# Reordering the first dense layer's first pass: contraction outermost over seven open banks, W1 in row slabs from two queues

## The chip, the cores and the metric

The kernel runs on one core of a Trainium2 chip. The core has a matrix engine (TensorE, PE in the profile; its weight loads are PEld), a vector engine (VectorE, DVE), an activation engine (ScalarE, ACT), a general engine (GpSimd, POOL) and a queue engine (SyncE, SP). Transfers are issued by SP, ACT and POOL and run on 16 DMA engines. The metric is the device time of one execution in microseconds: 227.01 us for the kernel before, the median of three runs (226.88 to 227.04).

## The reference

The input `x` has 2048 rows (time steps) of 640 columns in bf16. Two branches read it, and a gate mixes them row by row:

```
g   = sigmoid(sum(x * gate_w))                         # one number per row
# branch A: a diagonal complex recurrence over the 2048 rows
Bu  = x @ B_bar.T                                      # complex, 640 states
h_t = Lam_bar * h_{t-1} + Bu_t
a   = 2 * Re(h @ C.T) + x * Dskip
# branch B: a dense layer pair, 640 -> 1728 -> 640
b   = gelu(x @ w1 + b1) @ w2 + b2
out = g * a + (1 - g) * b
```

## The kernel before

**Tiling.** The 2048 rows are worked in four quarters q of 512. In each quarter there are four kinds of TensorE work. `m1(q)` (L612, matmuls in L622) multiplies W1 with the transposed x: the hidden dimension of 1728 is cut into NF = 14 groups of 128 (the last has 64), the contraction of 640 into KD = 5 blocks of 128. For each group `jf` five matmuls of 128x128 by 128x512 add into one PSUM bank of 512 columns, then ACT takes the bank through a gelu into `Gl` (L629). `bproj(q)` (L634, L643) does the same with the two parts of B: ten groups of five matmuls, which ACT evicts into `U` (L652). `m2` (L718) and `cproj` (L742) work on 128 rows each: the second dense layer from `Gl` and W2, and the output projection from the state `H` and C; ACT evicts both into `E1` and `E2`, VectorE adds them up and SP stores the rows. Between `bproj` and `cproj` VectorE runs the recurrence (`ssm`, L657) in blocks of 256 rows: products with tables that it builds at the start, a scan (L683), products again, giving `H`.

**PSUM.** There are eight banks. `m1` and `bproj` take banks 0 to 3 in rotation (`BK_IN`), `m2` banks 4 and 5, `cproj` banks 6 and 7. So `m1` closes a group, and moves on to the next bank, every five matmuls.

**Start.** The transposed x of the first quarter is made on TensorE: two loads of 256 rows each fill `xn[0]`, twenty transposes (L410, in four groups of five, one group per 128 rows) write it to PSUM, VectorE copies each group to `xT` (L418). The other three quarters of `xT`, and B and C, are loaded by transposing DMAs (`load_T`, L331). Seven matmuls on a zero tile (L388) run ahead of everything on TensorE. `cols` (L430) and `colb` (L442) transpose small parameter rows into columns; the bias column of the gelu, `b1col`, comes from `colb`. ACT loads a function table ahead of Exp, of Sin and of gelu.

**Loads.** SP issues, in this order: the two x loads, W1 in three column pieces (columns 0 to 256, 256 to 896, 896 to 1728, all 640 rows each), ten transposes of B, five transposes for the rest of `xT`, W2 in two pieces, ten transposes of C, then the stores. ACT issues five small loads. POOL issues b2, the broadcasts `dsk` and `gwb` (one row of 1280 bytes to all 128 partitions each), and x of the second quarter in untransposed form (`xnload`, L339), later the two other quarters.

**What sets the order.** Each piece of work is an `op` (L170) with an engine, an estimated duration, what it reads and writes, and a priority. `Sched.order` (L53) runs a list schedule in estimated time: on each engine the ready item of lowest priority number goes first. From it comes one fixed order for each engine. `Emitter.wait` (L116) puts semaphore waits in front of an item for what it depends on. An item that takes several instructions marks only its end.

Of the kernel before, what the change touches and what calls it, by code (L numbers as in the profile page):

```python
# [9 lines left out]
BF16 = mybir.dt.bfloat16  # L10
I32 = mybir.dt.int32
ACT = mybir.ActivationFunctionType
# [135 lines left out]
class Prog:  # L148
# [8 lines left out]
    def op(self, name, eng, dur, reads, writes, fn, prio=None, lat=0.0, after=()):  # L157
        deps = {}
        for k in reads:
            for w in self.last_w.get(k, ()):  # L160
                deps[w.idx] = w
        for k in writes:
            for w in self.last_w.get(k, ()):
                deps[w.idx] = w
            for r in self.last_r.get(k, ()):
                deps[r.idx] = r
        for a in after:
            deps[a.idx] = a
        deps = list(deps.values())
        E = self.E  # L170

        def run(eg, deps=deps, eng=eng, fn=fn):
            E.wait(eng, *[d.done for d in deps])
            return fn()

        it = self.sch.add(name, eng, dur, deps, run, prio=prio, lat=lat)
        for k in writes:
            self.last_w[k] = [it]
            self.last_r[k] = []
        for k in reads:  # L180
            self.last_r.setdefault(k, []).append(it)
        return it


def bass_gated_mix__ssm_conv_s5__dense_activation_gelu__prompt_kernel(
# [18 lines left out]
    _, S, D = A_x.shape  # L204
    P = A_Lambda_re.shape[0]
    F = B_w1.shape[1]
    assert S % 512 == 0 and D % 128 == 0 and P == D
    KD = D // 128
    KP = P // 128
    NQ = S // 512  # L210
# [3 lines left out]
    NF = (F + 127) // 128  # L214
    FL = F - (NF - 1) * 128
# [6 lines left out]
    x2 = A_x[0]  # L222
# [3 lines left out]
    with ExitStack() as es, nc.Block() as block:  # L226
# [4 lines left out]
        xT = SB("xT", [128, KD, S], BF16)  # L231
        xn = [SB(f"xn_{i}", [128, 4, D], BF16) for i in range(2)]
        W1sb = SB("W1sb", [128, KD, F], BF16)
        W2sb = SB("W2sb", [128, NF, D], BF16)
        BT = SB("BT", [128, KD, 2, P], BF16)
        CT = SB("CT", [128, KP, 2, D], BF16)
        Gl = [SB(f"Gl_{i}", [128, NF, 512], BF16) for i in range(2)]
        dsk = SB("dsk", [128, D], BF16)
        gwb = SB("gwb", [128, D], BF16)
        b1col = SB("b1col", [128, NF], FP32)  # L240
        rows = SB("rows", [KP, 3, 128], BF16)
        b1rows = SB("b1rows", [NF, 128], BF16)
        lcol = SB("lcol", [128, 3, KP], FP32)
# [8 lines left out]
        ident = SB("ident", [128, 128], BF16)  # L252
# [53 lines left out]
        def inc(eng, ins):  # L306
            return E.inc(eng, ins, eng + "_s")
# [8 lines left out]
        def d_act(n):  # L316
            return 0.26 + n * 0.00084
# [4 lines left out]
        def d_mm(n):  # L322
            return n / 2400.0 + 0.004


        def load(name, eng, sem, dst, src, writes, prio, dur=0.5, lat=2.5, reads=(), **kw):
            def fn():
                return dma_inc(eng, engines[eng].dma_start(dst, src), sem)  # L328
            return op(name, eng, dur, reads, writes, fn, prio=prio, lat=lat)

        def load_T(name, sem, pairs, writes, prio, dur, lat=3.0):  # L331
            def fn():
                t = None
                for dst, src in pairs:
                    t = dma_inc("sp", nc.sync.dma_start_transpose(dst, src), sem)
                return t
            return op(name, "sp", dur, (), writes, fn, prio=prio, lat=lat)
# [5 lines left out]

        for h in range(2):
            load(f"x0_{h}", "sp", f"l_x0{h}", xn[0][:, 2 * h:2 * h + 2, :],
                 x2[h * 256:(h + 1) * 256, :].rearrange("(c p) d -> p c d", p=128), [("xn", 0, h)], prio=h, lat=2.0 + h)
        W1P = [(0, 256), (256, 896), (896, F)]
        for i, (f0, f1) in enumerate(W1P):
            load(f"w1_{i}", "sp", f"l_w1{i}", W1sb[:, :, f0:f1], B_w1[:, f0:f1].rearrange("(k p) f -> p k f", p=128),
                 [("w1", i)], prio=2 + i, lat=3.0 + i)  # L350
        nmain = (NF - 1) * 128

        def f_b1z():
# [30 lines left out]

        def f_warm():
            t = None
            for _ in range(7):
                t = nc.tensor.matmul(PS[BK_C[1]][:, :], wz[:, 0:128], wz[:, :], start=True, stop=True)  # L388
            return inc("pe", t)

        op("warm", "pe", 3.0, ["wz"], [("bank", BK_C[1])], f_warm, prio=-1000)

        def f_ones():
            inc("dve", nc.vector.memset(Gl[0][64:65, NF - 1, :], 1.0))
            return inc("dve", nc.vector.memset(Gl[1][64:65, NF - 1, :], 1.0))

        op("ones", "dve", 1.1, (), ["gl1"], f_ones, prio=-40)
        load("b2", "pool", "l_b2", W2sb[64:65, NF - 1, :], B_b2.rearrange("(o n) -> o n", o=1), ["b2"], prio=-30, dur=1.0)
        load("dsk", "pool", "l_dsk", dsk[:, :], A_Dskip.partition_broadcast(128), ["dsk"], prio=-29, dur=1.0)
        load("gwb", "pool", "l_gwb", gwb[:, :], gate_w.partition_broadcast(128), ["gwb"], prio=-28, dur=1.0)  # L400


        for c in range(4):
            bank = BK_IN[c]

            def f_tp(c=c, bank=bank):
                ps = PS[bank][:, :].bitcast(BF16)
                t = None
                for k in range(KD):
                    t = nc.tensor.transpose(ps[:, k * 128:(k + 1) * 128], xn[0][:, c, k * 128:(k + 1) * 128], ident[:, :])  # L410
                return inc("pe", t)

            op(f"tp{c}", "pe", 0.5, [("xn", 0, c // 2), "ident"], [("bank", bank)], f_tp, prio=-900 + c)

            def f_tpe(c=c, bank=bank):
                ps = PS[bank][:, :].bitcast(BF16)[:, 0:KD * 128].rearrange("p (k t) -> p k t", k=KD)
                dst = xT[:, :, c * 128:(c + 1) * 128]
                return inc("dve", nc.vector.tensor_copy(out=dst, in_=ps))  # L418

            op(f"tpe{c}", "dve", 0.5, [("bank", bank)], [("xT", 0, c)], f_tpe, prio=-2000 + c)  # L420
        XT = {q: [("xT", q)] for q in range(1, NQ)}
        XT[0] = [("xT", 0, c) for c in range(4)]


        psC = PS[BK_C[0]][:, :].bitcast(BF16)

        def f_cols():
            t = None
# [1 line left out]
                t = nc.tensor.transpose(psC[:, i * 8:i * 8 + KP], rows[:, i, :], ident[0:KP, 0:KP])  # L430
            return inc("pe", t)

        op("cols", "pe", 0.3, [("rows", 0), ("rows", 1), ("rows", 2), "ident"], [("bank", BK_C[0])], f_cols, prio=-897.5)

        def f_cols1():
            return inc("dve", nc.vector.tensor_copy(out=lcol[:, :, :], in_=psC[:, 0:24].rearrange("p (a k) -> p a k", a=3)[:, :, 0:KP]))

        op("cols1", "dve", 0.2, [("bank", BK_C[0])], ["lcol"], f_cols1, prio=-1000)
        psD = PS[BK_M2[0]][:, :].bitcast(BF16)

        def f_colb():
            return inc("pe", nc.tensor.transpose(psD[:, 0:NF], b1rows[:, :], ident[0:NF, 0:NF]))  # L442

        op("colb", "pe", 0.1, ["b1a", "b1b", "ident"], [("bank", BK_M2[0])], f_colb, prio=-896)

        def f_colb1():
            return inc("dve", nc.vector.tensor_copy(out=b1col[:, :], in_=psD[:, 0:NF]))

        op("colb1", "dve", 0.2, [("bank", BK_M2[0])], ["b1col"], f_colb1, prio=-1000)

        def f_dt():
            return inc("act", nc.scalar.activation(dtb[:, :], lcol[:, 2, :], ACT.Exp))
# [115 lines left out]
        def f_atab():  # L568
# [4 lines left out]
        op("atab", "dve", 1.5, ["amag"], ["atab"], f_atab, prio=-946)  # L573


        load_T("xT_rest", "l_xT", [(xT[:, k, 512:S], x2[512:S, k * 128:(k + 1) * 128]) for k in range(KD)],
               [("xT", q) for q in range(1, NQ)], prio=7, dur=13.0)
        load_T("B", "l_B", [(BT[:, k, ci, :], (A_B_re, A_B_im)[ci][:, k * 128:(k + 1) * 128]) for k in range(KD) for ci in range(2)],
               ["BT"], prio=6, dur=13.1)
        load("w2a", "sp", "l_w2a", W2sb[:, 0:NF - 1, :], B_w2[0:nmain, :].rearrange("(j p) d -> p j d", p=128), ["w2a"], prio=8, lat=8.0)  # L580
        load("w2b", "sp", "l_w2b", W2sb[0:FL, NF - 1, :], B_w2[nmain:F, :], ["w2b"], prio=9, lat=4.0)
        load_T("C", "l_C", [(CT[:, k, ci, :], (A_C_re, A_C_im)[ci][:, k * 128:(k + 1) * 128]) for k in range(KP) for ci in range(2)],
               ["CT"], prio=10, dur=14.0)

# [2 lines left out]
        def pe_prio():  # L587
            ctr["pe"] += 1
            return ctr["pe"]
# [19 lines left out]
            op(f"g{q}", "dve", 0.3, [("gth", q)], [("g", q)], fn3, prio=-100)  # L609


        def m1(q):  # L612
            for jf in range(NF):
                bank = BK_IN[ctr["in"] % 4]
                ctr["in"] += 1
                n = 128 if jf < NF - 1 else FL
                wp = [i for i, (f0, f1) in enumerate(W1P) if f0 <= jf * 128 < f1][0]

                def f_mm(jf=jf, bank=bank, n=n):
                    t = None  # L620
                    for k in range(KD):
                        t = nc.tensor.matmul(PS[bank][0:n, :], W1sb[:, k, jf * 128:jf * 128 + n], xT[:, k, q * 512:(q + 1) * 512],  # L622
                                             start=(k == 0), stop=(k == KD - 1))
                    return inc("pe", t)

                op(f"m1_{q}_{jf}", "pe", KD * d_mm(512), XT[q] + [("w1", wp)], [("bank", bank)], f_mm, prio=pe_prio())

                def f_ge(jf=jf, bank=bank, n=n):
                    return inc("act", nc.scalar.activation(Gl[q % 2][0:n, jf, :], PS[bank][0:n, :], ACT.Gelu_apprx_tanh, bias=b1col[0:n, jf:jf + 1]))  # L629

                op(f"ge_{q}_{jf}", "act", d_act(512), [("bank", bank), "b1col"], [("gl", q % 2, jf)], f_ge, prio=10)
# [170 lines left out]
                cproj(c)  # L802
                comb(c)

        m1(0)
        bproj(0)
        ssm(0)
        gates(0)
# [84 lines left out]
```

## Time and profile before

The profiled execution took 227.38 us, with a span of 225.6 us from its first instruction to its last.

| engine | busy, us | share of the span |
|---|---|---|
| TensorE, matmuls | 218.3 | 97% |
| TensorE, weight loads | 124.8 | 55% |
| VectorE | 191.6 | 85% |
| ScalarE | 101.5 | 45% |
| GpSimd | 4.8 | 2% |

TensorE's matmul time by kind: `m1` 65.8 us (280 matmuls), `m2` 63.6 (448), `cproj` 46.1 (320), `bproj` 43.8 (200). A matmul's recorded duration is longer than its distance from the next one, since matmuls are pipelined; the distance is what counts in a stream. A busy share is an average over the whole span: the first 14 us of the span look unlike the rest, and the granted TensorE clock, shown as a share of full speed, is not the same throughout. HBM read 7.38 MB and written 2.62 MB.

### The profile page before, as it was taken

How to read it: one execution, taken by the hardware profiler on the slowest of the kernel's cores; microseconds unless marked ns; L12 is line 12 of the kernel's file. 1: busy time of each engine (PE TensorE's matmuls, PEld its weight loads, DVE VectorE, ACT ScalarE, POOL GpSimd, SP SyncE). 2: the span in 40 equal slices, each digit the busy share in tenths (PEclk: the TensorE clock that was granted, in tenths of full speed). 3: DMA queues.
4: the chain of work that ended last, by engine and by line, in shares of the span. 5: the costliest groups of instructions: out<-in, count | busy, mean ns of one | idle time of the engine just before them, and what ended most of it. 6: DMA issues, size and time to landing. Idle time of an engine off the chain costs nothing.

```text
span 225.6 us, 3268 instructions
## 1 busy us (share of the span) xinstructions
PE 218.3 (97%) x1279; PEld 124.8 (55%) x1279; DVE 191.6 (85%) x267; ACT 101.5 (45%) x170; POOL 4.8 (2%) x14
## 2 busy tenths in 40 slices
PE   7589999999999999999999999999999999999995
PEld 3224444444457777544447777644446777777773
DVE  4799999799996999999999559999999999894312
ACT  2385655666553233455663223455663332323320
POOL 5000000000000010000000010000000000000000
PEclk9659999999999999999999999999999999999999
DMA  5997699977100023000000003000000000000000
GB/s 165 314 260 150 121 202 237 292 146 99 29 0 3 29 48 127 32 0 0 0 3 0 31 32 116 29 29 0 3 0 3 0 29 32 29 29 32 29 29 29
DMA packets 28631, 15.44 MB, mean 68 GB/s; under 512 B 21834, under 2 KB 28170, under 8 KB 28618
## 3 DMA queue, kind: packets, MB, share of 16 engines
q1 hardware_dynamic: 28000, 12.95, 25.1%
q0 software_dynamic: 560, 2.30, 3.5%
q8 instruction: 10, 0.16, 0.3%
q14 instruction: 3, 0.02, 0.0%
q10 hardware_dynamic: 58, 0.01, 0.0%
HBM read 7.38 MB, written 2.62 MB: 44 GB/s over the span
## 4 chain that ended last, share of the span: by engine, by line
PE 93%; DMA 5%; SPq 1%; DVE 0%; issue 0%
PE ps L718 27%; PE ps L622 27%; PE ps L742 19%; PE ps L643 19%; DMA W1sb<-in_B_w_dram 5%; SPq L328 1%; DVE osb L775 0%
## 5 line engine op out<-in xcount | busy, mean ns | idle before, releaser
L622 PE MATMUL ps<-xT,W1sb 128*128 128x512 bf16 (+1 forms) x280 | 65.8, 397 | 1.8 <-DVE tr L474 1.1
L718 PE MATMUL ps<-W2sb,Gl 128*128 128x320 bf16 x448 | 63.6, 299 | 0.0
L718 PEld LDWEIGHTS ps<-W2sb,Gl 128*128 128x128 bf16 x448 | 43.6, 98 | 18.0 <-issue 0.8
L622 PEld LDWEIGHTS ps<-xT,W1sb 128*128 128x128 bf16 (+1 forms) x280 | 28.1, 102 | 38.7 <-issue 6.6
L629 ACT ACTIVATE Gl<-ps,b1col 128x512 bf16<-128x512 f32 (+1 forms) x56 | 38.5, 687 | 24.5 <-PE ps L622 24.5
L742 PE MATMUL ps<-CT,H 128*128 128x320 bf16 x320 | 46.1, 299 | 0.0
L683 DVE TENSOR_TENSOR_SCAN W<-atab,V 128x1280 bf16<-128x1280 f32 x16 | 44.3, 2811 | 0.3
L643 PE MATMUL ps<-xT,BT 128*128 128x512 bf16 x200 | 43.8, 379 | 0.0
L742 PEld LDWEIGHTS ps<-CT,H 128*128 128x128 bf16 x320 | 31.3, 98 | 12.3
L652 ACT ACTIVATE U<-ps 128x512 bf16<-128x512 f32 x40 | 23.9, 597 | 19.4 <-PE ps L643 19.4
L643 PEld LDWEIGHTS ps<-xT,BT 128*128 128x128 bf16 x200 | 19.4, 98 | 23.6 <-issue 0.8
L761 DVE SCALAR_TENSOR_TENSOR xg<-xn,gcol,dsk 128x640 bf16<-128x640 bf16 x16 | 14.0, 883 | 0.5
L726 ACT ACTIVATE E_0<-ps,g1col 128x320 bf16<-128x320 f32 x12 | 6.3, 527 | 16.5 <-PE ps L718 15.1
L596 DVE SCALAR_TENSOR_TENSOR scr<-xn,gwb 128x640 bf16<-128x640 bf16 x16 | 13.2, 823 | 0.4
L492 DVE TENSOR_TENSOR V<-mr,U 128x2560 bf16<-128x2560 bf16 x8 | 11.9, 1489 | 1.7 <-ACT U L652 1.5
L492 DVE TENSOR_TENSOR V<-V,W 128x1280 bf16<-128x1280 bf16 x16 | 12.5, 821 | 0.3
L492 DVE TENSOR_TENSOR H<-H,V 128x1280 bf16<-128x1280 bf16 x16 | 12.5, 821 | 0.3
L492 DVE TENSOR_TENSOR H<-c,W 128x2560 bf16<-128x2560 bf16 x8 | 11.9, 1489 | 0.2
L492 DVE TENSOR_TENSOR W<-mi,U 128x2560 bf16<-128x2560 bf16 x8 | 11.9, 1484 | 0.0
L492 DVE TENSOR_TENSOR V<-s,W 128x2560 bf16<-128x2560 bf16 x8 | 11.9, 1484 | 0.0
L726 ACT ACTIVATE E_1<-ps,g1col 128x320 bf16<-128x320 f32 x10 | 5.3, 528 | 13.7 <-PE ps L718 13.7
L726 ACT ACTIVATE E_2<-ps,g1col 128x320 bf16<-128x320 f32 x10 | 5.3, 527 | 13.7 <-PE ps L718 13.7
(87 smaller groups left out, 90.4 us busy)
## 6 DMA issues: line engine op xcount, KB each, us to landing
out_dram<-osb SPq DMA_DIRECT2D x15, 160.0 KB, 1.8
W2sb<-in_B_w_dram SPq DMA_DIRECT2D x1, 2080.0 KB, 10.8
xn<-in_A_x_dram POOLq DMA_DIRECT2D x3, 640.0 KB, 4.6
W1sb<-in_B_w_dram SPq DMA_DIRECT2D x1, 1040.0 KB, 13.7
W1sb<-in_B_w_dram SPq DMA_DIRECT2D x1, 800.0 KB, 11.6
xn<-in_A_x_dram SPq DMA_DIRECT2D x2, 320.0 KB, 3.3
W1sb<-in_B_w_dram SPq DMA_DIRECT2D x1, 320.0 KB, 6.9
dsk<-in_A_Dskip_dram POOLq DMA_DIRECT2D x1, 160.0 KB, 6.4
```

The source lines that it names most:

```text
L328: return dma_inc(eng, engines[eng].dma_start(dst, src), sem)
L492: return inc("dve", nc.vector.tensor_tensor(out=o, in0=a, in1=b, op=o_))
L596: t = inc("dve", nc.vector.scalar_tensor_tensor(out=scr[:, :], in0=xn[q % 2][:, c, :], scalar=1.0, in1=gwb[:, :], op0=ALU.mult, op1=ALU.mu ...
L622: t = nc.tensor.matmul(PS[bank][0:n, :], W1sb[:, k, jf * 128:jf * 128 + n], xT[:, k, q * 512:(q + 1) * 512], start=(k == 0), stop=(k == KD ...
L629: return inc("act", nc.scalar.activation(Gl[q % 2][0:n, jf, :], PS[bank][0:n, :], ACT.Gelu_apprx_tanh, bias=b1col[0:n, jf:jf + 1]))
L643: t = nc.tensor.matmul(PS[bank][:, :], BT[:, kd, ci, k * 128:(k + 1) * 128], xT[:, kd, q * 512:(q + 1) * 512], start=(kd == 0), stop=(kd = ...
L652: return inc("act", nc.scalar.activation(dst, src, ACT.Copy, scale=1.0 if ci == 0 else -1.0))
L683: t = inc("dve", nc.vector.tensor_tensor_scan(out=g[:, ci, :], data0=a, data1=v[:, ci, :], initial=0.0, op0=ALU.mult, op1=ALU.add))
L718: t = nc.tensor.matmul(PS[bank][:, 0:HALF], Gl[q % 2][0:n, jf, t4 * 128:(t4 + 1) * 128], W2sb[0:n, jf, cols], start=(jf == 0), stop=(jf == ...
L726: return inc("act", nc.scalar.activation(E1[c % NE][:, cols], PS[bank][:, 0:HALF], ACT.Copy, scale=g1col[:, c:c + 1]))
L742: t = nc.tensor.matmul(PS[bank][:, 0:HALF], H[b % NHB][:, ci, k, s * 128:(s + 1) * 128], CT[:, k, ci, cols], start=(i == 0), stop=(i == 2 ...
L761: return inc("dve", nc.vector.scalar_tensor_tensor(out=xg[c % 2][:, :], in0=xn[q % 2][:, c % 4, :], scalar=gcol[:, c:c + 1], in1=dsk[:, :] ...
```

## The change

The first quarter's `m1` is split. `m1_first` does hidden groups 0 to 6 with the contraction block `k` as the outer loop: for each `k`, seven matmuls, one into each of banks 0 to 6, so that seven groups are open at once and all close in the last round. Groups 7 to 13 follow as before (`m1(0, NW)`). W1's columns 0 to 896 come as five row slabs of 128 rows, one for each `k`; slabs 0, 2, 4 on SP's queue, 1 and 3 on ACT's; the rest of W1 is one load on SP. The transposes of x are grouped by `k` rather than by rows, so that each bank holds one `k`; three of the five copies to `xT` are VectorE's and two ScalarE's. The zero-tile matmuls ahead become six instead of seven, and two more are put after each half of the transposes (`filler`). `colb` moves behind the second slab's matmuls. `b2`, `dsk` and `gwb` are issued only after the first matmul of slab 1 (`late`), which leaves POOL's x load as its first. On SP, the transposes of x are cut in two (the second quarter, then the third and fourth), and W2 goes between them. On VectorE, the gates of the first quarter fall behind the building of the tables. The other three quarters keep their form.

```diff
-        W1P = [(0, 256), (256, 896), (896, F)]
-        for i, (f0, f1) in enumerate(W1P):
-            load(f"w1_{i}", "sp", f"l_w1{i}", W1sb[:, :, f0:f1], B_w1[:, f0:f1].rearrange("(k p) f -> p k f", p=128),
-                 [("w1", i)], prio=2 + i, lat=3.0 + i)
+        NW = 7
+        FW = NW * 128
+        for k in range(KD):
+            load(f"w1_{k}", "sp" if k % 2 == 0 else "act", f"l_w1{k}", W1sb[:, k, 0:FW], B_w1[k * 128:(k + 1) * 128, 0:FW],
+                 [("w1", k)], prio=2 + k if k % 2 == 0 else -97.5 + 0.1 * k, lat=2.6 + 0.5 * k)
+        load("w1_r", "sp", "l_w1r", W1sb[:, :, FW:F], B_w1[:, FW:F].rearrange("(k p) f -> p k f", p=128), [("w1", "r")], prio=6.5, lat=5.0)
...
-            for _ in range(7):
-                t = nc.tensor.matmul(PS[BK_C[1]][:, :], wz[:, 0:128], wz[:, :], start=True, stop=True)
+            for _ in range(6):
+                t = nc.tensor.matmul(PS[6][:, :], wz[:, 0:128], wz[:, :], start=True, stop=True)
...
+        def filler(name, n, prio, deps):
+            def fn():
                 t = None
+                for _ in range(n):
+                    t = nc.tensor.matmul(PS[6][:, :], wz[:, 0:128], wz[:, :], start=True, stop=True)
                 return inc("pe", t)
+            op(name, "pe", n * 0.22, ["wz"] + deps, [("bank", 6)], fn, prio=prio)
+
+        for h in range(2):
+            for k in range(KD):
+
+                def f_tp(k=k, h=h):
+                    ps = PS[k][:, :].bitcast(BF16)
+                    t = None
+                    for c in (2 * h, 2 * h + 1):
+                        t = nc.tensor.transpose(ps[:, c * 128:(c + 1) * 128], xn[0][:, c, k * 128:(k + 1) * 128], ident[:, :])
+                    return inc("pe", t)
+
+                op(f"tp{h}{k}", "pe", 0.13, [("xn", 0, h), "ident"], [("bank", k)], f_tp, prio=-900 + 20 * h + k)
+            filler(f"fill{h}", 2, -890 + 20 * h, [("xn", 0, h)])
+        for k in range(KD):
+
+            def f_tpe(k=k):
+                src = PS[k][:, :].bitcast(BF16)[:, 0:512]
+                dst = xT[:, k, 0:512]
+                if k % 2 == 0:
+                    return inc("dve", nc.vector.tensor_copy(out=dst, in_=src))
+                return inc("act", nc.scalar.activation(dst, src, ACT.Copy))
+
+            op(f"tpe{k}", "dve" if k % 2 == 0 else "act", 0.5, [("bank", k)], [("xT", 0, k)], f_tpe, prio=-2000 + k)
...
-        op("colb", "pe", 0.1, ["b1a", "b1b", "ident"], [("bank", BK_M2[0])], f_colb, prio=-896)
+        op("colb", "pe", 0.1, ["b1a", "b1b", "ident"], [("bank", 7)], f_colb, prio=14.5)
...
-        load_T("xT_rest", "l_xT", [(xT[:, k, 512:S], x2[512:S, k * 128:(k + 1) * 128]) for k in range(KD)],
-               [("xT", q) for q in range(1, NQ)], prio=7, dur=13.0)
+        for nm, a, e in (("xT1", 1, 2), ("xT23", 2, NQ)):
+            load_T(nm, "l_" + nm, [(xT[:, k, a * 512:e * 512], x2[a * 512:e * 512, k * 128:(k + 1) * 128]) for k in range(KD)],
+                   [("xT", q) for q in range(a, e)], prio=6 + a, dur=4.4 * (e - a))
...
-               ["BT"], prio=6, dur=13.1)
+               ["BT"], prio=6.8, dur=13.1)
...
+        def m1_first():
+            for k in range(KD):
+                for jf in ((5, 6, 0, 1, 2, 3, 4) if k == 0 else range(NW)):
+
+                    def f_mm(jf=jf, k=k):
+                        return inc("pe", nc.tensor.matmul(PS[jf][:, :], W1sb[:, k, jf * 128:(jf + 1) * 128], xT[:, k, 0:512],
+                                                          start=(k == 0), stop=(k == KD - 1)))
+
+                    op(f"m1_0_{jf}_{k}", "pe", d_mm(512), [("xT", 0, k), ("w1", k)], [("bank", jf)] + (["late"] if (k, jf) == (1, 0) else []),
+                       f_mm, prio=pe_prio())
+            for jf in range(NW):
+
+                def f_ge(jf=jf):
+                    return inc("act", nc.scalar.activation(Gl[0][:, jf, :], PS[jf][:, :], ACT.Gelu_apprx_tanh, bias=b1col[:, jf:jf + 1]))
+
+                op(f"ge_0_{jf}", "act", d_act(512), [("bank", jf), "b1col"], [("gl", 0, jf)], f_ge, prio=10)
...
-        m1(0)
+        m1_first()
+        load("b2", "pool", "l_b2", W2sb[64:65, NF - 1, :], B_b2.rearrange("(o n) -> o n", o=1), ["b2"], prio=-30, dur=1.0, reads=["late"])
+        load("dsk", "pool", "l_dsk", dsk[:, :], A_Dskip.partition_broadcast(128), ["dsk"], prio=-29, dur=1.0, reads=["late"])
+        load("gwb", "pool", "l_gwb", gwb[:, :], gate_w.partition_broadcast(128), ["gwb"], prio=-28, dur=1.0, reads=["late"])
+
+        m1(0, NW)
```

## The prediction

> **What bounds the kernel now.** I read the chain of work that ended last first. From 13.91 us it is TensorE without a gap; before that stand 11.6 us of waiting for a piece of W1.
>
> ```profile
> 2.27 11.59 DMA W1sb<-in_B_w_dram
> 13.86 0.05 issue
> 13.91 15.23 PE ps L622 x60
> 29.14 10.90 PE ps L643 x50
> 40.04 15.22 PE ps L622 x70
> ...
> 69.97 2.72 PE ps L742 x20
> ...
> 222.91 0.55 DVE osb L775
> ```
>
> A full-speed matmul of 512 columns costs 15.22/70 = 0.2174 us. The 60 at 13.91 should have taken 13.04 and took 15.23. So the end is set by when TensorE gets into its stream, and how fast it then runs. The timeline shows what happens before, the windows why some of it is slow (columns after the span of time: PE, PEld, DVE, ACT, POOL busy and counts; then granted clock, DMA share, GB/s).
>
> ```profile
> 1.20 3.17 PE L388 MATMUL ps<-wz 128*128 128x512 bf16 x7 [1.20 <-DVE wz L381]
> ...
> 4.16 1.28 PE L410 MATMUL ps<-ident,xn 128*128 128x128 bf16 x15
> ...
> 8.76 4.42 PE L622 MATMUL ps<-xT,W1sb 128*128 128x512 bf16 x10 [1.07 <-DVE tr L474]
> ```
>
> ```profile
> 5.00:7.00 2.00, 0.99 (x13) 0.68 (x13) 1.52 (x5) 0.21 (x1) 0.00 (x0) 1.00 0.80 138
> 7.00:8.00 1.00, 0.18 (x1) 0.09 (x1) 0.27 (x3) 0.00 (x0) 0.00 (x0) 0.87 0.99 301
> 8.00:13.00 5.00, 4.24 (x10) 1.31 (x10) 4.68 (x13) 3.39 (x4) 0.00 (x0) 0.50 1.03 393
> 13.00:17.00 4.00, 3.27 (x9) 1.17 (x9) 3.79 (x21) 3.30 (x6) 0.00 (x0) 0.50 1.25 203
> 17.00:18.00 1.00, 1.00 (x4) 0.32 (x3) 0.90 (x10) 0.00 (x0) 0.00 (x0) 0.51 0.87 189
> ```
>
> The clock falls to half at about 7.7 (0.87 in the slice 7 to 8) and comes back at about 17.97; there a matmul costs 0.427 us. Between these, TensorE idles from 13.0 to 13.91 for the second piece. The landings, by the DMA issues (last column: us from issue to landing, a median where x2):
>
> ```profile
> W1sb<-in_B_w_dram SPq DMA_DIRECT2D x1, 1040.0 KB, 13.7
> W1sb<-in_B_w_dram SPq DMA_DIRECT2D x1, 800.0 KB, 11.6
> xn<-in_A_x_dram SPq DMA_DIRECT2D x2, 320.0 KB, 3.3
> W1sb<-in_B_w_dram SPq DMA_DIRECT2D x1, 320.0 KB, 6.9
> dsk<-in_A_Dskip_dram POOLq DMA_DIRECT2D x1, 160.0 KB, 6.4
> ```
>
> With the issue times that gives: x0 3.7 and 4.94, first W1 piece 8.67, second 13.86, third 16.51. The slices 5 to 7 move only 138 GB/s against 393 from 8 to 13: the two broadcasts (dsk, gwb) are being read then, and the first W1 piece is behind them.
>
> **The change, part by part.** The reference point is the first B-projection matmul, at 29.07 now; from there TensorE runs the same instructions in the same order in both kernels.
>
> *Loads.* SP's queue carries x0 twice (640 KB), slabs 0, 2, 4 (224 KB each), then the rest of W1 (1040 KB); ACT's queue carries slabs 1, 3, issued behind three small loads that end at 1.95 now. The broadcasts leave this stretch. But POOL's 640 KB load of the next x, issued at 3.22 behind b2, dsk and gwb, is now POOL's first and goes out near 1.5. The x0 halves arrived at some 300 GB/s while alone. If the added queue and the early x load take nothing from it, the second half still lands at 4.9. [...] Sharing packet by packet (some 290 KB of x0 left when slab 1 begins near 3.1, the x load from 3 to 4) I get 5.9 to 6.9. I take 6.3, as now two queues beside one another total 393 GB/s, not more. [...] All bytes through slab 0 behind x0 (x0 640, slabs 0, 1, 3 672, x load 640 KB) at 370 to 390 GB/s from the first bytes at 1.85 end at about 7.1, landed 7.6. Slabs 2 and 4 follow 0.6 us apart (8.3, 8.9), the rest of W1 lands at 11.7.
>
> *Entry.* After the second x0 half at 6.3: ten transposes at 0.056 to 0.107 us (the 15 now took 1.28), two filler matmuls (0.43 to 0.85), during which VectorE copies three of the five transposed tiles (0.41 to 0.49 each; 0.486 for 640 columns now) and ACT two (0.60, the row of U copies). First real matmul: 6.3 + 0.56 + 0.43 = 7.3 to 8.2, slab 0 at 7.6: I take 7.7.
>
> *Clock.* [...] So I take full speed from 11.15.
>
> *The sum.* From 7.7 to 11.15: 3.45/0.427 = 8.1 matmuls. The other 61.9 of 70: x 0.2174 = 13.46, so 24.6. Now 29.07: 4.5 us gained.
>
> *Gelu.* The seven banks fill together. ACT works seven gelus of 0.69 us in a row from about 15.9 and the eighth ends at about 21.4, while the matmul that reuses its bank wants 16.96 + 4 x 1.08 = 21.3: 0.2 us lost, bounds 0 and 0.7. Its table and the bias column (copied after the slab-1 matmuls at 12.5) are ready at about 14. Waits of each of the 35 matmuls on one seven before: nothing, that one ended 1.5 us ago (15.22/70 already includes such waits at each group).
>
> *B, behind SP.* The projection needs all ten B transposes.
>
> ```profile
> 3.64 7.64 SPq L335 DMA_TRANSPOSE BT<-in_A_B_re_dram  x1
> 11.33 2.20 SPq L335 DMA_TRANSPOSE BT<-in_A_B_im_dram  x1
> 13.57 2.68 SPq L335 DMA_TRANSPOSE BT<-in_A_B_re_dram  x1
> 16.29 1.27 SPq L335 DMA_TRANSPOSE BT<-in_A_B_im_dram  x1
> ```
>
> The first three are held up until W1 has drained (16.0); then 1.31 us each, the last landing at 27.0, 2 us before its use. Unmoved, B would cap the gain at 2.0. But W1 drains by 11.1 now to come, which puts B at 27.0 - 4.9 = 22.2, plus the broadcasts: POOL issues b2, dsk, gwb (0.65 + 0.59 + 0.54) after slab 1's first matmul at about 10.9, so they read from 13 to 16, in the middle of B, and cost it 1 us (0 to 2.2, the width of the slow slices). B: 23.2, hidden behind 24.6.
>
> *Further on SP.* Ten x transposes for five (bound 0 to 3 us more issue), W2 between them, C last: landed at 58.2, used at 69.97, 65.6 in future. Hidden. POOL's next load waits until 82 anyway.
>
> *VectorE.* The gates (3.4 us at 11.2 now, in a wait) move behind the table building, since gwb is late; the tables start 2 us earlier. Its first scan stage then starts near 39 (40.7 now, 1.5 of it waiting for U), the first H is ready near 56 as now and is needed at 65.6; the second, 71 against 78.5. Slack shrinks from 11.7 to 7 and holds.
>
> Sum: 4.5 - 0.2 = 4.3. The profiled run had a span of 225.6 in 227.38 us, so 221.3 in 223.1; the median of the runs is 227.01, hence **222.7 us**.
>
> **Rivals.**
> 1. *The clock stays up* at 7.73, fillers being enough, or x0 lands at 5: 7.7 + 70 x 0.2174 = 22.9, capped by B at 23.2; 221.4. Against: the present drop under similar work.
> [...]
> 3. *B lands late* (broadcasts cost it the same again or the queue holds it as now): 26 to 27, and over 2 us of idle may drop the clock for a window (1.7): 225 to 226.8. For it: the queue hold of 7.64 us.
> [...]
>
> **How the numbers follow.** Main case 0.50, rival 1 0.15, rival 2 0.17, rival 3 0.07, slower 0.11. Main and the first two are faster: 0.82, and most of rival 3, 0.04; the measurement tells 0.2% (0.45 us) from nothing. Faster 0.86, same 0.03, slower 0.11. Main alone 222.0 to 223.4. The range holds rivals 1 and 2 with the bounds of B and gelu: 220.9 to 225.6.
>
> **What would show it.** First first-layer matmul near 7.7; clock back near 11.2; no W1 wait in the chain; B projection from about 24.6 without a wait on BT; from there pieces as long as now. Wrong if the granted clock is 0.50 after 15, if the chain holds a wait for BT, or if VectorE's H is waited for.

## The result and the profile after

The changed kernel takes 224.30 us (median of four runs, 224.06 to 224.63) beside 227.02 (226.88 to 228.4) of the kernel before on the same chip: a ratio of 0.9867 [0.9827, 0.9908], or 2.7 us less. A repeat on another chip gives 224.58 (six runs, 223.19 to 224.83), ratio 0.9864 [0.9833, 0.9895]. The forecast was 222.7 with a range of 220.9 to 225.6: the direction and the range hold, but 4.3 us were expected and 1.6 of them are missing. Runs over 1.5% above the fastest of the same kernel are left out of all ratios; here that sets aside two runs of e9 (227.11 and 229.75 us) and one of e7 (226.37).

The first profiled execution took 224.63 us with a span of 222.8. Its chain of work that ended last (start, length, what):

```profile
1.26 6.83 DMA xn<-in_A_x_dram
8.08 0.04 issue
8.13 1.12 PE ps L416 x10
9.25 0.85 PE ps L405 x2
10.10 3.89 PE ps L628 x14
13.98 0.11 PE ps L452
14.09 4.64 PE ps L628 x21
18.73 7.67 PE ps L649 x35
26.41 10.90 PE ps L670 x50
37.30 15.23 PE ps L649 x70
...
220.18 0.55 DVE osb L802
```

The wait for W1 (11.6 us) is gone from the chain. In its place stands the second half of x0 (the first quarter's x), landed at 8.08 us, and after it TensorE has no gap. The B projection (L670) starts at 26.41 where it started at 29.14, and 29.14 - 26.41 = 2.73 is the whole gain: from there the pieces are as long as before (10.90, 15.23). The windows of this execution, with the same columns as in the prediction, show two things:

```profile
1.80:5.00 3.20, 3.20 (x17) 1.77 (x15) 0.97 (x4) 1.28 (x1) 0.55 (x1) 1.00 0.91 270
5.00:8.00 3.00, 0.60 (x6) 0.14 (x3) 0.17 (x1) 0.21 (x1) 0.00 (x0) 1.00 0.96 335
8.31:11.72 3.41, 3.41 (x17) 1.71 (x15) 3.09 (x11) 2.83 (x5) 0.00 (x0) 0.50 1.04 395
11.72:16.00 4.28, 4.28 (x22) 1.82 (x21) 2.97 (x14) 1.61 (x3) 1.63 (x3) 1.00 1.11 212
```

The clock is at half for 3.41 us (8.31 to 11.72; a stretch of that length is called a half-speed window below), where it was for 10.24 us in the kernel before (7.73 to 17.97). And until 8 us the loads come in at 270 and 335 GB/s, some 300 on the mean; only then at 395. The loads, by the DMA issues (last column: us from issue to landing, a median where there are several):

```profile
W1sb<-in_B_w_dram SPq DMA_DIRECT2D x1, 1040.0 KB, 10.3
W1sb<-in_B_w_dram SPq DMA_DIRECT2D x3, 224.0 KB, 8.0
xn<-in_A_x_dram SPq DMA_DIRECT2D x2, 320.0 KB, 4.8
W1sb<-in_B_w_dram ACTq DMA_DIRECT2D x2, 224.0 KB, 8.0
```

By their landing times slab 0 is there at 9.19, slabs 2 and 4 at 10.27 and 10.92, the rest of W1 at 13.54; the second quarter's x (the x load, from here on) on POOL's queue at 9.77. B's transposes on SP's timeline:

```profile
3.83 4.63 SPq L335 DMA_TRANSPOSE BT<-in_A_B_re_dram  x1
8.50 1.79 SPq L335 DMA_TRANSPOSE BT<-in_A_B_im_dram  x1
10.33 2.93 SPq L335 DMA_TRANSPOSE BT<-in_A_B_re_dram  x1
13.31 1.27 SPq L335 DMA_TRANSPOSE BT<-in_A_B_im_dram  x1
...
21.18 2.18 SPq L335 DMA_TRANSPOSE BT<-in_A_B_im_dram  x1
```

The third is held until 13.26, the last is issued at 21.18, and B is complete at 25.95. TensorE was free for B at about 26.2. So the two met within 0.3 us in this execution, and the weight loads of the projection show a wait of only 0.4 us for B:

```profile
L670 PEld LDWEIGHTS ps<-xT,BT 128*128 128x128 bf16 x200 | 19.4, 98 | 23.6 <-DMA BT<-in_A_B_im_dram 0.4
```

The profile of the repeat, e13 below, tells them apart. There x0 was complete at 4.95, so TensorE started earlier, and waited for B instead. Its timeline of TensorE:

```profile
8.17 1.67 PE L628 MATMUL ps<-xT,W1sb 128*128 128x512 bf16 x7 [1.37 <-DVE tr_i L486]
10.09 1.69 PE L628 MATMUL ps<-xT,W1sb 128*128 128x512 bf16 x7 [0.24 <-DMA W1sb<-in_B_w_dram]
...
16.36 7.83 PE L649 MATMUL ps<-xT,W1sb 128*128 128x512 bf16 x35
26.24 10.97 PE L670 MATMUL ps<-xT,BT 128*128 128x512 bf16 x50 [2.05 <-DMA BT<-in_A_B_im_dram]
```

Its chain of work that ended last runs through B's transposes:

```profile
21.67 4.52 DMA BT<-in_A_B_im_dram
26.24 10.97 PE ps L670 x50
```

The first layer's pass ends near 24.2, and then 2.05 us are spent waiting for B, which lands at 26.20. (The 1.37 us ahead of the first matmul are put down to a VectorE item; slab 0, at 8.04, was the last to come.) The two executions start 1.7 us apart, at 9.89 and 8.17, and enter the B projection 0.1 us apart. In the repeat B sets the entry. In the first the late x0 and a half-speed window brought TensorE to the projection 0.3 us after B: there the start set it, and that the two entries agree so closely is chance.

### The profile page after: what moved, and what is told of

Read it like the earlier page. It is cut to its first block, busy times and chain, and to the rows that moved or that the text cites. A ratio compares the mean times of both kernels' runs of the same rounds, so it can differ in the third digit from the quotient of the medians.

```text
span 222.8 us, 3280 instructions
## 1 busy us (share of the span) xinstructions
PE 216.4 (97%) x1282; PEld 125.1 (56%) x1282; DVE 190.4 (85%) x266; ACT 100.5 (45%) x171; POOL 4.8 (2%) x14
## 4 chain that ended last, share of the span: by engine, by line
PE 95%; DMA 3%; DVE 0%; SPq 0%; issue 0%
PE ps L745 27%; PE ps L649 24%; PE ps L769 20%; PE ps L670 19%; PE ps L628 4%; DMA xn<-in_A_x_dram 3%; PE ps L416 1%; PE ps L405 0%; DVE osb L802 0%; SPq L328 0%; PE ps L452 0%
## 5 line engine op out<-in xcount | busy, mean ns | idle before, releaser
L649 PE MATMUL ps<-xT,W1sb 128*128 128x512 bf16 (+1 forms) x245 | 54.0, 379 | 0.0
L670 PE MATMUL ps<-xT,BT 128*128 128x512 bf16 x200 | 43.8, 379 | 0.0
L656 ACT ACTIVATE Gl<-ps,b1col 128x512 bf16<-128x512 f32 (+1 forms) x49 | 33.4, 693 | 18.1 <-PE ps L649 18.1
L649 PEld LDWEIGHTS ps<-xT,W1sb 128*128 128x128 bf16 (+1 forms) x245 | 23.9, 99 | 29.5 <-issue 1.7
L670 PEld LDWEIGHTS ps<-xT,BT 128*128 128x128 bf16 x200 | 19.4, 98 | 23.6 <-DMA BT<-in_A_B_im_dram 0.4
L753 ACT ACTIVATE E_0<-ps,g1col 128x320 bf16<-128x320 f32 x12 | 6.4, 530 | 16.4 <-PE ps L745 16.4
```

The lines of the kernel that those rows point to most:

```text
L670: t = nc.tensor.matmul(PS[bank][:, :], BT[:, kd, ci, k * 128:(k + 1) * 128], xT[:, kd, q * 512:(q + 1) * 512], start=(kd == 0), stop=(kd = ...
L753: return inc("act", nc.scalar.activation(E1[c % NE][:, cols], PS[bank][:, 0:HALF], ACT.Copy, scale=g1col[:, c:c + 1]))
```

## The experiments

The theory after the result: the start works about as forecast, and B, which was to be hidden, is the new bound. Rivals: the clock, the loops over the contraction, the second queue, the broadcasts in the middle of B, the early x load. Each experiment is named by its label (e1 to e13). Each run's ratio is to the kernel before on the same chip; that one took 227.39, 227.71 and 227.48 us in the three groups of runs.

### B without its transposes (e12_b_plain)

```diff
-        load_T("B", "l_B", [(BT[:, k, ci, :], (A_B_re, A_B_im)[ci][:, k * 128:(k + 1) * 128]) for k in range(KD) for ci in range(2)],
-               ["BT"], prio=6.8, dur=13.1)
+                t = dma_inc("sp", nc.sync.dma_start(BT[:, :, ci, :], (A_B_re, A_B_im)[ci].rearrange("(k p) d -> p k d", p=128)), "l_B")
```

> The changed kernel with B loaded by two plain loads in place of ten transposing ones (so B stands untransposed and the projection's numbers are another matrix's; the work on every engine is the same). Theory (the last B transpose is what the changed kernel meets next): B lands near 15, TensorE goes into the projection when the first layer is done, at 24.4 with full clock or 26.1 with one half-clock window: 222.0 to 222.8 in runs of mean clock 1.0, 224 in one with the drop. Rival (entry alone sets the end, B was hidden): 224.0 to 224.6 as the changed kernel, clock or no clock.

B is loaded untransposed by two plain loads, so the projection multiplies with another matrix; the work of the engines is unchanged, and the x transposes behind B come earlier too. Measured: 222.37 us (222.08 to 222.59), ratio 0.9752 [0.9721, 0.9783]. B is complete at 19.27, and TensorE's timeline shows the entry with no wait for it:

```profile
8.13 3.33 PE L633 MATMUL ps<-xT,W1sb 128*128 128x512 bf16 x14 [0.94 <-DMA W1sb<-in_B_w_dram]
...
24.04 10.74 PE L675 MATMUL ps<-xT,BT 128*128 128x512 bf16 x49 [0.16 <-issue]
```

No other wait of TensorE follows, here or in the repeat. So B's lateness costs the changed kernel about 224.5 - 222.4 = 2 us, the 2.05 us of the repeat's wait. The forecast's entry (24.6) and time (222.7) are met within 0.6 and 0.3 us, but with the clock at full speed in all four runs, where the forecast had counted one half-speed window; how its terms moved is told below.

### The next x not ahead of the slabs (e1_xload_late)

```diff
-        xnload(1, "g")
+        xnload(1, "g", reads=["late"])
```

> The changed kernel, with the POOL load of the second quarter's x (640 KB) issued behind b2, dsk and gwb, after slab 1's first matmul, instead of first. Theory (the x load delays the second x0 half, and the last B transpose is the next bound): second x0 half lands at 6 us instead of 8.1, first first-layer matmul at 8 instead of 9.9; but B now shares with the x load and lands at 26 to 27, so TensorE waits for BT and the time stays at 224 to 225. Rival (only the entry counts, B is hidden): 222.3.

Only the x load moves here. Measured: 225.17 us (224.98 to 225.83), ratio 0.9904 [0.9874, 0.9935]: no gain on the changed kernel. The start did get better: second half of x0 at 4.78, first matmul 7.17, first layer's pass done at 22.8. SP's third B transpose is released earlier as well, at 8.46 + 2.94 = 11.40 instead of 13.26:

```profile
8.46 2.94 SPq L335 DMA_TRANSPOSE BT<-in_A_B_re_dram  x1
```

But the 640 KB now come in the middle of B (one B issue on SP takes 3.28 us instead of 1.27), B lands at 25.13, and TensorE stands still for it. Timeline and windows:

```profile
25.40 12.43 PE L670 MATMUL ps<-xT,BT 128*128 128x512 bf16 x49 [2.62 <-DMA BT<-in_A_B_im_dram]
```

```profile
22.80:25.40 2.60, 0.00 (x0) 0.11 (x2) 2.53 (x3) 0.68 (x1) 0.00 (x0) 1.00 0.59 125
25.40:26.50 1.10, 1.10 (x6) 0.51 (x6) 1.10 (x2) 0.03 (x1) 0.00 (x0) 1.00 0.52 116
26.50:29.91 3.41, 3.41 (x10) 1.17 (x9) 3.34 (x3) 1.16 (x2) 0.00 (x0) 0.50 0.59 77
```

After 2.60 us of idling the clock is at half for 3.41 us, and 49 matmuls take 12.43 us instead of 10.74: 1.7 us more. What an earlier start had won was lost once to the wait and once to the clock behind it. It is rival 3 of the prediction in full, in this execution.

### The broadcasts behind B (e9_bcast_after_b)

```diff
-    [("bank", jf)] + (["late"] if (k, jf) == (1, 0) else []),
+    [("bank", jf)],
...
+    [("bank", bank)] + (["late"] if (q, jf) == (0, 11) else []), f_mm, prio=pe_prio())
```

> The changed kernel with b2, dsk and gwb issued after group 11 of the first quarter (near 22 us), past most of B's transposes; the x load stays first on POOL. Theory: B lands 1 to 2 us earlier, 24 to 25, time 222.8 to 223.6. Rival (broadcasts cost B nothing, or B is hidden): 224.0 to 224.6.

`b2`, `dsk` and `gwb` now go out after hidden group 11. The two runs that count took 223.07 and 225.02 us, ratio 0.9826 [0.9758, 0.9895], which does not separate it from the changed kernel. In the trace of the latter B lands at 26.69, no earlier than before and not at 24 to 25 as expected, and TensorE waits longest of all. POOL's timeline shows where the broadcasts went:

```profile
26.96 10.74 PE L670 MATMUL ps<-xT,BT 128*128 128x512 bf16 x49 [2.87 <-DMA BT<-in_A_B_im_dram]
```

```profile
22.64 0.57 POOL L328 DMA_DIRECT2D dsk<-in_A_Dskip_dram  x1
23.21 0.54 POOL L328 DMA_DIRECT2D gwb<-in_gate_w_dram  x1
```

The edit clears them from the middle of B and sets them beside its last transpose (issued at 21.86), so it does not free B of them. The forecast had given them 1 us of B's time, and the repeat shows that they are not what makes B late: there they had landed by 16.4, and the last transpose, issued at 21.67, still took 4.5 us.

### POOL's loads behind W1 and most of B (e4_all_clear, e10_x_last)

```diff
-            load(f"w1_{k}", "sp" if k % 2 == 0 else "act", ...)
+            load(f"w1_{k}", "sp", ...)
...
-    (["late"] if (k, jf) == (1, 0) else [])
+    (["late"] if (q, jf) == (0, 11) else [])
...
-        xnload(1, "g")
+        xnload(1, "g", reads=["late"])
```

All five slabs go on SP's queue, and `b2`, `dsk`, `gwb` and the x load wait for hidden group 11. e10 is the same, with the x load behind the second quarter's B projection.

> The changed kernel with all five slabs on SP's queue and all four POOL loads (b2, dsk, gwb, x) issued only after group 11 of the first quarter. Theory: second x0 half at 4.9 as before the change, first first-layer matmul at 6.6, W1 drained by 10, B landed near 21, entry to the B projection at 22 (full clock) to 23.5 (one half-clock window), time 220 to 221.4. Rival (entry set by slabs or by the clock for two windows more): over 223.

> The kernel of the all-clear run (slabs on SP alone, b2, dsk, gwb after group 11) with the x load put off further, to the end of the second quarter's projection. Theory: B lands at 23.2 as there, the wait of 0.5 us for the second quarter's x transposes goes, C isn't late: 220.5 to 221.2. Rival (the x load's bytes are late for something else, or C lands past its use): 222 or more.

Measured: e4 221.47 us (220.85 to 223.56), ratio 0.9751 [0.9683, 0.9819]; e10 223.18 (221.65 and 221.84 with the clock full throughout, 224.53 twice at a mean of 0.992), ratio 0.9786 [0.9715, 0.9858]. e4 is near its forecast of 220 to 221.4; e10 misses its forecast of 220.5 to 221.2. In e4's timeline of TensorE

```profile
7.61 3.20 PE L628 MATMUL ps<-xT,W1sb 128*128 128x512 bf16 x14
...
23.48 10.74 PE L670 MATMUL ps<-xT,BT 128*128 128x512 bf16 x49 [0.25 <-DMA BT<-in_A_B_im_dram]
34.69 5.56 PE L649 MATMUL ps<-xT,W1sb 128*128 128x512 bf16 x25 [0.47 <-DMA xT<-in_A_x_dram]
```

the wait for B is 0.25 us. B lands at 23.21 here, 2 us later than expected, and at 23.33 in e10; SP's third B transpose is released at 11.86 rather than 13.26. The x load comes against the next transposes instead (0.47 us for `xT` in e4). With the x load ahead of the slabs, B landed between 25.26 and 26.69 in seven such profiles of the changed and near kernels (the changed twice, e2, e6b, e7, e9, and e5), at 27.32 in e6, and at 25.13 with the x load in B's midst (e1). The edits that e4 makes besides are shown alone by e9 (broadcasts: 26.69) and e2 (slabs on one queue: 25.5). So what brings B forward by 2 to 3 us is that the 640 KB of the next x are out of the way. e1, which moves them alone, shows the first part: the third transpose goes out 1.9 us earlier. The rest is the last transpose's time from issue to landing, 3.4 us in e4 and 4.77 in the changed kernel. That part can't be given to the x load: with the load first on POOL it was anything from 2.9 (e2) to 4.8 (e9). The x load was not run alone behind B.

### One queue for the slabs (e2_slabs_sp)

```diff
-            load(f"w1_{k}", "sp" if k % 2 == 0 else "act", ...)
+            load(f"w1_{k}", "sp", ...)
```

> The changed kernel with all five slabs on SP's queue, the x load still first on POOL. If the second queue brings nothing (same engines, interleaved): slab 0 lands earlier (6.5 to 7 instead of 8.0), slab 4 at 10 to 11 as now, B as now, time 224.0 to 224.8. If two queues move the slabs faster: slab 4 lands 1 us or more later, time over 225.

Measured: 223.64 us (223.03 to 225.43) beside 224.58 (223.19 to 224.83) for the changed kernel in the same group of runs: ratios 0.9842 [0.9801, 0.9882] and 0.9864 [0.9833, 0.9895], not separated. Slab 0 lands at 7.91 (6.5 to 7 was expected) and slab 4 at 11.23, the first matmul is at 8.32, B at 25.5. The second queue is worth nothing that shows. In the packet records of the changed kernel's first profile the three queues take turns: from 5 to 8 us SP's moves 202 KB, ACT's 228 and POOL's 545, together at 335 GB/s, beside 324 in e4 (also 5 to 8 us), where SP's queue carries the slabs alone and POOL's loads are not out yet.

### No filler matmuls (e7_no_filler)

```diff
-            filler(f"fill{h}", 2, -890 + 20 * h, [("xn", 0, h)])
```

> The changed kernel without the four filler matmuls behind the transposes (six warm matmuls stay). Theory (fillers help to keep the clock up through the window from about 5 to 8.4, in which the clock fell once in four runs of the changed kernel): mean clock 0.985 to 0.992 in most runs; since B lands at 26 anyway one half-clock window (1.7 us) fits into the wait and the time is 224.3 to 225. If fillers do nothing: clock 1.0 in most runs, 224.3.

Measured: 224.98 us (222.15 to 226.37), ratio 0.9856 [0.9808, 0.9904]. In the profile x0 is complete at 6.53, the first matmul is at 9.19, and the B projection starts at 26.46 without a wait for B (25.26). The first matmuls follow one another by 0.427 us until 12.56, which is half speed, and TensorE's timeline shows it too:

```profile
9.19 4.92 PE L627 MATMUL ps<-xT,W1sb 128*128 128x512 bf16 x14 [1.37 <-DVE tr L483]
```

Fourteen take 4.92 us where e12, e4 and e11 need 3.2 to 3.3. That says that the clock was half here and full in those, and in the changed kernel's first profile half again (9.89 to 11.6). TensorE was busy for 40% of 5.91 to 9.33, and for 60% of 5.11 to 8.52 in the repeat, which has the fillers and whose clock stayed full; but x0 also came 1.6 us later here. So whether the fillers help the clock can't be read from so few; the time does not show them.

### The late loads without the new loop (e5_before_bcast_late)

The kernel before, with one edit: `b2`, `dsk` and `gwb` go out after group 0 of `m1(0)`. That leaves the x load first on POOL's queue here too.

```diff
-                op(f"m1_{q}_{jf}", ..., [("bank", bank)], f_mm, prio=pe_prio())
+                op(f"m1_{q}_{jf}", ..., [("bank", bank)] + (["late"] if (q, jf) == (0, 0) else []), f_mm, prio=pe_prio())
```

> The kernel before with one thing of the change: b2, dsk and gwb are issued after the first group's matmuls. Theory (the order of the loads is the gain, the loop order is not): the first W1 piece lands near 7.5 instead of 8.67 and the second near 11 instead of 13.86, no gap at 13, B near 26, time 223.5 to 225. Rival (contraction-outermost makes the gain): 226.5 to 227.

Measured: 224.80 us (223.91 to 226.09), ratio 0.9887 [0.9840, 0.9935]. With three column pieces and groups of five, TensorE's timeline reads:

```profile
8.12 2.32 PE L619 MATMUL ps<-xT,W1sb 128*128 128x512 bf16 x10 [1.27 <-DVE tr L471]
10.61 13.50 PE L619 MATMUL ps<-xT,W1sb 128*128 128x512 bf16 x59 [0.17 <-DMA W1sb<-in_B_w_dram]
25.77 10.74 PE L640 MATMUL ps<-xT,BT 128*128 128x512 bf16 x49 [1.67 <-DMA BT<-in_A_B_im_dram]
```

The second piece comes at 10.56 and not at 13.86, the first layer's pass ends at 24.1, and B (25.5) is waited for. In the repeat of the changed kernel the pass ended at 24.2 and B landed at 26.20. Putting the broadcasts behind the start gives, alone, about all that the change gives.

### The row slabs without the new loop (e6_group_outer, e6b_old_groups)

```diff
-        m1_first()
+        m1(0)
...
-        m1(0, NW)
```

This is e6b: slabs and loads as changed, groups of five as before. e6 instead keeps one item per matmul, and swaps the two loops of `m1_first`. In both the late loads wait for the end of a whole group, the first in e6b and the last of the pass in e6.

> The changed kernel with the first pass's 35 matmuls in the old nesting (group outer, contraction inner, groups 5, 6, 0 to 4), slabs and loads as changed; the later loads go out after the last group's last matmul (some 4 us later), since their marker sits there. Theory: all slabs have landed by 10.9, the fifth is wanted at 11.6, so the loop order is worth nothing by itself; the broadcasts fall later into B, B lands within 1 us of 26: 223.5 to 224.5. Rival (the loop order is the gain): 225.5 to 227.

> The changed kernel with the first pass in its old form (groups of five matmuls, marked at their end only, banks 0 to 3 in rotation), slabs, loads and transposes as changed. In place of the earlier group-outer run, where each of the 35 matmuls waited for the one before it in the same bank. Theory: the pass starts when the last slab lands, 11 to 12, instead of 8.6 to 9.9 with slab 0: the loop order is worth 1 to 2 us at the entry; 70 x 0.217 from 11.5 is 26.7, or 28.4 with a half-clock window: 225 to 226.5. Rival (B at 26 is the bound whatever the entry): 224.0 to 224.8.

Measured: e6b 227.08 us (ten runs, 226.36 to 228.41), ratio 0.9980 [0.9954, 1.0006]; e6 231.23 (230.57 to 231.85), 1.0165 [1.0128, 1.0203]. Both are slower than was expected (225 to 226.5 and 223.5 to 224.5). e6b's timeline and windows:

```profile
11.82 17.05 PE L649 MATMUL ps<-xT,W1sb 128*128 128x512 bf16 x69 [0.28 <-DVE acol L467]
29.02 10.74 PE L670 MATMUL ps<-xT,BT 128*128 128x512 bf16 x49 [0.16 <-issue]
```

```profile
4.00:11.80 7.80, 2.98 (x28) 1.97 (x28) 1.49 (x7) 2.10 (x4) 0.00 (x0) 1.00 0.96 333
11.80:15.22 3.42, 3.40 (x9) 1.22 (x10) 3.20 (x11) 3.19 (x5) 0.80 (x2) 0.50 1.21 229
```

A group of five needs all five slabs, and the fifth lands at 11.55, so the pass starts at 11.82, after a long gap and at half clock. (`colb`, ahead of it, waited until 11.36 for its own rows, which ACT issues behind the two slabs; the slab came last.) The slabs are worth nothing without the loop that uses them one by one, and that loop is worth 227.1 - 224.5, some 2.6 us, given the slabs, with the gap and its half-speed window in that sum. e6 failed as a test of the nesting. It measures something else, as its waits say:

```profile
PEld ps L628 <- PE ps L628: 10.9, 23, 1.0
```

Each matmul into the same bank waited for the one before it, since here every one is an item with its own wait: the weight loads idled 10.9/23 = 0.47 us each for it, and at full clock the matmuls of one group start 0.45 us apart (18.00, 18.45, 18.89, 19.34).

### The best version (e11_rest_on_act), and the changed kernel again

e10 with the rest of W1 on ACT's queue:

```diff
-        load("w1_r", "sp", ..., prio=6.5, lat=5.0)
+        load("w1_r", "act", ..., prio=-95, lat=5.0)
```

> The all-clear kernel with the x load last, and the rest of W1 (1040 KB) on ACT's queue, so that SP comes to B's transposes right behind the slabs. Theory (B's start is set by what drains ahead of it on SP): the first B transposes go out by 8, B lands at 21 to 22.5, TensorE reaches the projection without a wait at 22.7 to 23, clock stays, 220.3 to 221.3 with little scatter. Rival (the transposes are slowed as much by the W1 traffic beside them): B at 23 or later, 221.5 to 224.5 with the scatter of the run before.

> The changed kernel once more, on the chip of the next three, unedited. If the second x0 half's landing at 8.1 us in the first profile was that execution's own (five profiles of kernels with the same first loads, or nearly so, show 4.6 to 4.8), it lands near 4.7 here, the first first-layer matmul stands near 8.1, TensorE waits 1 to 2.5 us for B and the time is 224 to 225 all the same. If the x load and ACT's slabs hold x0 up as a rule: 6 to 8 again.

Measured: e11 221.37 us (six runs, 220.93 to 222.37), ratio 0.9736 [0.9706, 0.9765], the clock at 0.999 or 1.0 in all. It beats both kernels: 6.1 us below the one before and 3.2 below the changed one in the same group of runs (224.58; its profile was shown with the result). Its timeline:

```profile
6.81 3.18 PE L628 MATMUL ps<-xT,W1sb 128*128 128x512 bf16 x14 [0.17 <-DMA W1sb<-in_B_w_dram]
...
22.90 10.97 PE L670 MATMUL ps<-xT,BT 128*128 128x512 bf16 x50 [0.49 <-DMA BT<-in_A_B_im_dram]
```

Slab 0 is there at 6.68, the first layer's pass ends at 22.4, B at 22.86. Start and B are both early and within half a microsecond of each other. The time is at the edge of its forecast (220.3 to 221.3), while B came later than expected (21 to 22.5). Beside e10's better runs (221.65, 221.84) the queue of the last W1 load adds little or nothing; that the slower e10 runs are at 0.992 and none of e11's is may be chance in so few.

## Why the prediction was right, and where it was wrong

- **Entry: near as a sum, by terms that moved, so in part by luck.** Forecast: x0's second half 6.3, slab 0 7.6, first matmul 7.7, B projection 24.6. Measured: x0 at 8.08 in one execution and 4.95 in the other, slab 0 at 9.19 and 8.04, first matmul 9.89 and 8.17, TensorE free for B at 26.2 and 24.2; with B out of the way 24.04. That last figure is near only because errors cancel: the start was 0.4 late, the half-speed window (1.7) did not come, and 0.7 went into short gaps that the sum did not hold (24.6 + 0.4 - 1.7 + 0.7 = 24.0). The early x load is paid for, but x0 does not always pay: with the x load first, x0 landed anywhere from 4.6 to 8.1 in eight profiles with slabs, in five of them below 5, while slab 0 always came at 7.8 to 9.2. With the x load put off, slab 0 came at 6.5 to 7.0 (e1, e4, e10, e11).
- **Clock: not the same in every run, as was assumed, and without effect on the time.** Forecast: half speed from 7.73 to 11.15. No run shows the 11.15, from which the sum has its 8.1 matmuls at half speed. Measured: half from 8.31 to 11.72 in the first profile, full throughout in the repeat's. Of ten runs three have a mean clock of 0.992, which is one half-speed window (0.5 x 3.41/222.7 = 0.0077), and seven 0.999 or 1.0; those seven are an upper bound (see the last section). So the forecast's clock and rival 1's both occur. It made no difference to the time of these runs: in the repeat the runs at 0.992 took 224.16 and 224.64, the four others 223.19 to 224.83. A half-speed window ahead of B only filled the wait for B (0.4 us of it were left in the first profile, 2.05 in the repeat). One behind it cost 1.7 us (e1). TensorE was busy for 26% of the 3.41 us before the fall in the first profile, which waited for x0, and for 60% of 5.11 to 8.52 in the repeat, where the clock stayed full. The fall did not keep its place either: 7.73 in the profile before, 8.31 in the one after.
- **B "23.2, hidden behind 24.6": this is the step that failed.** Measured 25.95 and 26.20, which is 2.75 and 3.0 late; TensorE was left to wait 1.6 to 2.9 us in the profiles where it came early. Its first term was the drain of W1, put at 11.1 from 370 to 390 GB/s. The rate until 8 us was (3.2 x 270 + 3 x 335)/6.2 = 301, so some (380 - 301) x 6.2 = 490 KB were left, 1.2 us at 395; the last W1 packet ended at 13.0, 1.9 late, of which 0.7 stays unexplained. SP's third B transpose was released at 13.26, not at 16.25 - 4.9 = 11.35, and the last was so issued 1.9 late (21.18, not 19.27). The second term was the end: 2.85 us from the last issue to its landing before, and 1 for the broadcasts. It took 4.77. So 23.2 + 1.9 + 0.9 = 26.0. The 1 us given to the broadcasts was the wrong cause: in the repeat they were long in and it still took 4.5. It is 2.9 to 4.8 in the profiles with the x load first (2.9 in e2, 3.6 in e7) and 3.4 to 3.7 in those without (e1, e4, e10, e11). Why that last stretch differs stays open.
- **Rival 3 was what happened**, at its place (the wait for BT) and without its second half: the clock dropped in e1 after 2.6 us of idling (half speed for 3.41 us, 1.7 us lost), not in the repeat after 2.05, and not in e9 after 2.87. By the prediction's own sign ("if the chain holds a wait for BT") the repeat shows its main path wrong. Rival 3 at 225 to 226.8 was priced with B at 26 to 27 and, at its upper end, the clock's 1.7. With B at 26.2 and a full clock: 222.7 + 26.3 - 24.6 = 224.4, and 224.3 was measured. That lies below rival 3's own span and inside the stated range, whose ends were drawn for rivals 1 and 2: that the range held is luck. Rival 3 had a chance of 0.07, with the hold of 7.64 us on SP's queue named as evidence: too little. The 1.4 us between the forecast start (24.6) and B (23.2) were less than the 1.7 by which rival 1 moves the start (to 22.9); and B's bound, 22.2 to 24.4, covered the broadcasts alone and not the drain.
- **No W1 wait in the chain, nothing else lost after the entry: right.** Rival 2 and the slower case did not come: full speed was back at 11.72 in the first profile and never lost in the repeat, and the slabs arrive about as fast as they are used (one wait of 0.24 us in the repeat).
- **Gelu: 0.2 allowed, none seen.** The seven gelus took 4.16 us, 0.59 each where 0.69 was taken.
- **VectorE's slack: right.** The second block's H is ready at 72.7 and used from 80.3, forecast 71 against 78.5; TensorE waits nowhere after the entry.
- **What the gain is made of.** The forecast did not part the slabs and the loop from the new order of the loads. e5 shows that moving the two broadcasts away from the first W1 piece yields about the same with the old loop, and e6b that the slabs alone yield nothing. With the x load first, all good starts meet the same wall, B at 25.3 to 26.7.

## What to carry to other kernels

When a change removes a wait at the start, ask which transfer is due next and cost it by its own queue: what stands ahead of it, at the rate the loads really had in that stretch, and its own time to land. Two ends that lie closer than the error of each are to be treated as a coin toss, not as "hidden". A load that is needed late (here x of the next quarter, 640 KB) belongs behind the loads that are due first; to move it from the start into the middle of the next due transfer gains nothing, and a wait on TensorE may cost a half-speed window on top: it did in e1 (2.60 us of waiting, 1.7 us lost to the clock behind it), not in the repeat (2.05) nor in e9 (2.87).

## What the runs showed of the hardware that was not expected

- The kernel before does not have one fixed start: its mean clock was 0.977 to 0.992 in its runs, one to three half-speed windows of 3.41 us by that mean (0.977 is the profile with 10.24 us at half speed). Other kernels scatter too (e10: 221.65 and 221.84 at full clock, 224.53 twice at 0.992). One half-speed window is 1.7 of those 2.8 us; no profile of the slower runs was kept, so the rest is open.
- Two pauses of like length ended differently. In e1 TensorE stood still for 2.60 us (22.80 to 25.40), was busy for 32% of 23.09 to 26.50, and the clock was at half from 26.50 to 29.91. In e9 it stood still for 2.87 us (24.09 to 26.96), was busy for 53% and 63% of the stretches below, and the clock stayed full.

```profile
23.09:26.50 3.41, 1.10 (x6) 0.62 (x8) 3.38 (x3) 0.45 (x2) 0.00 (x0) 1.00 0.57 125
```

```profile
22.28:25.69 3.41, 1.81 (x8) 0.56 (x6) 3.34 (x4) 1.63 (x3) 1.47 (x3) 1.00 0.82 151
25.69:29.10 3.41, 2.14 (x10) 1.09 (x12) 3.38 (x3) 0.60 (x1) 0.00 (x0) 1.00 1.11 166
```

Among stretches of 3.41 us at the start, 26% busy (the first profile, 4.89 to 8.31) and 40% (e7, 5.91 to 9.33) came before half speed, 49% (e2, 4.70 to 8.11) and 60% (the repeat, 5.11 to 8.52) before full. But the kernel before lost the clock after 53% (4.32 to 7.73), nearly all of it transposes, so these shares do not settle it. What makes the clock fall was not shown; no run was made to find it.

- The granted clock in the records missed a half-speed window at the start of e7's profile: the slice from 9.33 to 12.74 reads 1.00, while its matmuls came 0.427 us apart, as they do at 0.50 in the kernel before. Where it matters, read the distance of the matmuls.
- A transposing issue of B on SP took 1.27 us at the least, and up to 3.28 in the middle of B (e1, while POOL's x load was being read). That the x load caused it is not shown: e2 has one of 2.24 (at 18.97) after all POOL loads had landed.
- Matmuls that add to the same bank, each waiting by a semaphore for the one before, went 0.45 us apart (e6), against 0.217 in a plain stream, where each matmul's record lasts 0.379 and they overlap.
